# Moving GpSimd's scaling of v behind VectorE's sums, and state copies behind a bank copy, in a fused attention and MLP kernel

## The chip, the cores and the metric

One core of a Trainium2 chip runs the whole program in one launch. The metric is the device time of that core in microseconds (us); the page and the traces count from the start of the profiled span.

## The reference

A causal linear attention with a decay per head, in blocks, followed by an MLP with the exact GELU:

```python
# q, k, v: (4, 8, 768, 64); lam: (8,), 0.97 to 0.99; blocks of 64 positions
for b in range(nb):
    intra = einsum(einsum(qb, kb) * Dmask, vb)       # Dmask = lam ** (i - j) for i >= j
    inter = einsum(qb * lam_pow, kv_state)           # lam_pow = lam ** (pos + 1)
    out[block] = intra + inter
    kv_state = lam ** 64 * kv_state + einsum(kb * lam ** (63 - pos), vb)
x = out as (3072 tokens, 512)
h = x @ w_in                                         # w_in: (512, 2048)
result = gelu(h) @ w_out                             # w_out: (2048, 512)
```

## The kernel before

**Tiling.** The 768 positions of the 4 batches are cut into 24 chunks of 128 positions, numbered so that four chunks in a row are the same positions of the four batches. Four chunks make a group: group 0 to 5, each 512 tokens of the MLP. While the MLP of group g runs on TensorE, the attention of the chunks of group g + 1 is fitted in between, so that its output `xT[g + 1]` is there when the next group begins.

**The MLP of a group** (from group 1 on) saves matmuls by forming seven products where eight are needed, at the price of sums and differences. In `first_blocks`, the first layer:

- `los` and `his` are plain blocks (L643) on the low and high half of the tokens, and `x` and `y` two `Step` objects of seven products each (L426).
- Products 4 to 7 read `x_s[4]`, `x_s[1]`, `x_s[2]` and `x_s[3]`: differences of parts of x, made by `x_sums` on VectorE (L402). Both inputs of these four steps lie in SBUF.
- ScalarE copies a product's bank out (`kept`, L432), VectorE adds the next product to it from the bank (`total`, L435), ScalarE applies the GELU (L438, L646).
- A bank is used again: for instance products 6, 7 and 4 of a step go into `ha` one after the other, each behind the copy or add that reads the one before.

In `blocks_by_seven`, the second layer, products m1, m2, m5, m6, m3, m7, m4 are made twice (u = 0 and 1, L535). m1, m6, m7 and m4 use bank a; ScalarE copies it out behind m1, m6 and m7 (`f_p`, `f_u`, L567) and behind m4 (L620). `g_sum` (L516) are VectorE's sums of the GELU's outputs, again from SBUF to SBUF. The blocks m3 and m7 stand in the order m3 0, m7 0, m7 1, m3 1, m4 0.

**The attention of a pair of chunks.** Loads of k, q and v are issued on GpSimd's DMA queue (`load`, L69 and L72); k and q are transposed by DMA from SyncE's queue (`dma_transposes`, L181, L182); GpSimd scales v by powers of lam (`decay_v`, L160, giving `v_dec`). On TensorE a pair has a *visit* (`pair_visit`): first the states' part of the answer for the pair `done` (L314), then the scores (L279) and the products of k and v (L290) for the pair `asked`, then the values' part (L326) for `done`. Behind the visit VectorE adds the products to the states (`mid_states` L296, `end_states` L301), masks the scores (`mask`, L305, from PSUM into `sc_m`), scales the sum of the states (`new_states`, L240, from SBUF to SBUF) and empties the answers into x (`empty_half`, L333). ScalarE reorders some states (`reorder_states`, four copies, L229).

**What sets the order.** Every engine runs its instructions in the order in which the program lists them. The blocks of the MLP give the line of time: their cost is counted in columns that TensorE streams. Each step of the attention is put on a list with a place on that line, and before each block of the MLP everything whose place has come is issued, to all engines:

```python
            while todo and todo[0][0] <= done:
                todo.pop(0)[1]()
            run()
            done += cost
```

A place is written as group plus a part of it: `g + 4 * B` is group g and four units further. One unit B is a block of 2048 columns, such as one of `los`; a group has 29 of them. A step that waits holds back all that stands behind it on its engine. For GpSimd this means that v_decs and the loads behind them stand in one line.

In group 1 the v_decs of chunks 8, 9 and 10 are issued around the start of the group (`begin_at`), ahead of the loads of chunk 12. In groups 2 to 4 they are issued at 1 B or 7 B, with new states at 9.5 B and 10.5 B and masks at 4 B. Eight semaphores serve GpSimd's loads in turn, so a load also waits until the one eight places ahead of it has landed. The tile of v has 8 buffers, `v_dec` 6, k 10 and q 8.

Of the kernel before, what the change touches and what calls it, by code (L numbers as in the profile page):

```python
# [9 lines left out]
BF16 = mybir.dt.bfloat16  # L10
# [5 lines left out]
def kernel(  # L16
# [10 lines left out]
    nc = tc.nc  # L27

    B, H, S, D = q.shape
# [10 lines left out]
    M = 4  # L40
# [5 lines left out]
    consts = ctx.enter_context(tc.tile_pool(name="consts", bufs=1))  # L46
# [104 lines left out]
    def begin(n, early=False):  # L151
        c = Chunk()
        c.n, c.sb, c.early = n, n // M, early
        c.q, c.k, c.v = (raw.pop((n, name)) for name in "qkv")
        return c

    def decay_v(c, eng):

        c.v_dec = work_pool.tile([128, H, D], BF16, tag="vd", name="v_dec", bufs=6)
        eng.tensor_mul(c.v_dec, c.v, lam_m[:, :, None].to_broadcast((128, H, D)))  # L160
# [17 lines left out]
    def dma_transposes(c):  # L178
        c.kT = work_pool.tile([128, HP, C], BF16, tag="kT", name="kT", bufs=4)
        c.qT = work_pool.tile([128, HP, C], BF16, tag="qT", name="qT", bufs=6)  # L180
        nc.sync.dma_start_transpose(out=c.kT, in_=c.k.rearrange("p h d -> p (h d)"))  # L181
        nc.sync.dma_start_transpose(out=c.qT, in_=c.q.rearrange("p h d -> p (h d)"))  # L182
# [199 lines left out]
    def w_in_sums(*which):  # L382
        lo, hi = (w_in_t[:, :, (k0 + KW[0]) * 128:(k0 + KW[0] + NW) * 128] for k0 in (0, KH))
        for i in which:
# [3 lines left out]
                        4: lambda: (lo[:, 2:], w_in_s[2], ALU.subtract)}[i]()  # L388
            nc.vector.tensor_tensor(w_in_s[i], a, b, op=op)

    def first_blocks(g, g_t, x_t, mm1):

        TH = M * C // 2
        lo, hi = slice(0, TH), slice(TH, 2 * TH)
        x_s = {}

        def x_sums():
            for i in (1, 2, 3, 4):
                x_s[i] = sum_pool.tile([128, 2, TH], BF16, tag=f"x{i}", name=f"x_sum{i}")
                a, b = {1: lambda: (x_t[:, :2, hi], x_t[:, :2, lo]), 2: lambda: (x_t[:, 2:, hi], x_s[1]),  # L400
                        3: lambda: (x_t[:, 2:, hi], x_t[:, :2, hi]), 4: lambda: (x_t[:, 2:, lo], x_s[2])}[i]()
                nc.vector.tensor_sub(x_s[i], a, b)  # L402
# [74 lines left out]
        x, y = Step(KW[0]), Step(KW[2])  # L477
        x.behind, y.ahead = y, x

        def then_sums(run):  # L480
            def both():
                x_sums()
                run()
            return both

        los = [mm1(kf, 2, lo) for kf in (0, KH, 2, KH + 2)]
        his = [mm1(kf, 2, hi, tag) for kf, tag in ((0, "t"), (KH, "o"), (2, "t"), (KH + 2, "mh"))]
        if g > 1:
            los[2] = then_sums(los[2])
        plain = 4 * 2 * TH  # L490
        plan = [(run, plain) for run in los]
        plan += [(then_sums(x.p1) if g == 1 else x.p1, plain // 2), (his[0], plain)]
        plan += [(x.p2, plain // 2), (x.p5, plain // 2), (his[1], plain)]
        plan += [(run, plain // 2) for run in (x.p6, x.p3, y.p1, x.p7, y.p2, y.p5, y.p6, x.p4, y.p3)]
        plan += [(his[2], plain), (y.p7, plain // 2), (his[3], plain), (y.p4, plain // 2)]
# [137 lines left out]
    def mlp_blocks(g):  # L633
# [31 lines left out]
        if g > 0:  # L665
            return blocks_by_seven(g, g_t, first_blocks(g, g_t, x_t, mm1))
# [26 lines left out]
    live = {}  # L693
# [104 lines left out]
    def at(when, run):  # L798
        todo.append((place(when), run))

    def begin_at(when, n):
        def run():
            live[n] = begin(n)
            dma_transposes(live[n])
            decay_v(live[n], nc.gpsimd)
        at(when, run)

    totals = {}
# [59 lines left out]
    def visit_at(when, done, asked, *then, **how):  # L868
        at(when, lambda: visit(done, asked, **how))
        for step in then:  # L870
            w, run = when, step[0]
            if isinstance(run, float):
                w, step = run, step[1:]
            at(w, lambda step=step: step[0](*step[1:]))

    B = 2 * M * 2 * C / later

    def begun(*chunks):
        for n in chunks:
            live[n] = begin(n)  # L880
# [17 lines left out]
    visit_at(1, [], [2 * M - 2, 2 * M - 1], (masks, 2 * M - 1, 2 * M - 2),  # L898
             (w_in_sums, 4, 3), banks="t o")
    visit_at(1 + 4 * B, [2 * M - 2, 2 * M - 1], [], (empties, 2 * M - 2, 2 * M - 1), (sums, M, M + 2),  # L900
             (1 + 9.5 * B, new_states, M), (1 + 10.5 * B, new_states, M + 2), states_of=(M, M + 2), kv_tags="sc sc")
    n = 2 * M
    steps((1 + 7 * B, prefetch, 3 * M + 1), (1 + 11 * B, prefetch, 4 * M - 1),
          (1 + 15 * B, pair_visit, None, n, "t o"), (1 + 16 * B, mid_states, n), (1 + 16 * B, end_states, n),
          (1 + 16 * B, mask, n, 0), (1 + 16 * B, mask, n, 1),
          (1 + 19 * B, pair_visit, n, n + 2, "mh mo", nc.scalar.copy), (1 + 23 * B, mid_states, n + 2),
          (1 + 23 * B, end_states, n + 2), (1 + 24 * B, empty_half, n, 0), (1 + 25 * B, empty_half, n, 1),
          (1 + 25 * B, new_states, n), (1 + 25 * B, reorder_states, n + M),
          (1 + 25 * B, mask, n + 2, 0), (1 + 25 * B, mask, n + 2, 1),
          (1 + 16 * B, decayed, n + M, n + M + 1, n + M + 2, n + M + 3), (1 + 16 * B, prefetch, 4 * M),  # L910
          (1 + 26 * B, prefetch, 4 * M + 1))
    for g in range(2, NG):
        n = (g + 1) * M
        done, asked = n - 2, n if g < NG - 1 else None
        early = (g + 1 * B, empty_half, done, 0), (g + 1 * B, empty_half, done, 1)
        if not asked:
            steps((g, begin_answers, done, nc.vector.tensor_copy), (g + 1 * B, end_answers, done), *early)
            break
        v = g + 1 * B
        steps((v, pair_visit, done, asked), *[(v, *e[1:]) for e in early], (v, mid_states, asked))  # L920
        if asked < NCH - M:
            steps((v, end_states, asked), (g + 9.5 * B, new_states, asked))
        if done < NCH - M:
            steps((g + 10.5 * B, new_states, done))
            if done < N_UP:
                steps((g + 16 * B, reorder_states, done + M))
        steps((g + 4 * B, mask, asked, 0), (g + 4 * B, mask, asked, 1))
        if g > 2:
            steps((g + 7 * B, decays, n + 2, n + 3))
        if g < NG - 2:  # L930
            if g > 2:
                steps((g + 1 * B, prefetch, n + M + 1))
            steps((g + (7 if g > 2 else 1) * B, decayed, n + M, n + M + 1), (g + 8 * B, prefetch, n + M + 3),
                  (g + 26 * B, begun, n + M + 2, n + M + 3))
        done, asked = n, n + 2
# [13 lines left out]
    done = 0  # L949
# [42 lines left out]
```

## Time and profile before

| | before |
|---|---|
| runs | 201.25, 201.5, 205.04 us; median 201.5 |
| profiled execution | 202.12 us, its span 200.3 us |
| granted TensorE clock | 0.995 |
| TensorE busy | 189.9 us (95%) |
| VectorE busy | 135.4 us (68%) |
| ScalarE busy | 105.5 us (53%) |
| GpSimd busy | 111.0 us (55%) |

In the profile PE is TensorE's matmuls, DVE is VectorE, ACT is ScalarE, POOL is GpSimd and SPq SyncE's queue. A row of a time line gives start and duration in us, the engine, the line of the kernel, the operation, what it writes and reads, the shape and a count; in brackets stands how long the engine sat idle before it, and what it waited for. Neighbouring instructions of one kind are merged into one row. A row of DMA issues gives the size and the us from issue to landing.

### The profile page before, as it was taken

To read this page: it belongs to the slowest core of one execution; us is meant where nothing else is said; L and a number is where in the kernel's file an instruction comes from. 1 tells how busy PE (TensorE), PEld (TensorE's weight loads), DVE (VectorE), ACT (ScalarE), POOL (GpSimd) and SP (SyncE) were. 2 spreads that over 40 slices of the span, in tenths; PEclk is the share of its full clock that TensorE was granted. 3 is DMA by queue.
4 is the path that set the end of the run, shared out by engine and by line. 5 is a ranking of instruction groups with operands and counts; after the bars stand their busy time and mean duration, and the time that the engine had idled before them with its cause. 6 is when DMAs were issued, how large, how long until landed. Compare 5 with 4: busy or idle time off the path is not lost.

```text
span 200.3 us, 6454 instructions
## 1 busy us (share of the span) xinstructions
PE 189.9 (95%) x2800; PEld 154.3 (77%) x2804; DVE 135.4 (68%) x220; ACT 105.5 (53%) x205; POOL 111.0 (55%) x136
## 2 busy tenths in 40 slices
PE   7899999999989998899899989999999999999991
PEld 2478674455878887788798878898888898888880
DVE  3753504867888899488897499889577694555830
ACT  4954564234559614358923258812379522589221
POOL 8999973689957999499299971972000000000000
PEclk9999999999999999999999999999999999999997
DMA  4999999999999999999989999899500000500005
GB/s 113 151 174 176 200 204 201 157 212 151 133 207 134 154 137 139 142 251 143 106 53 117 158 279 139 56 104 111 213 0 5 0 3 23 190 3 0 0 3 209
DMA packets 102764, 24.81 MB, mean 124 GB/s; under 512 B 93264, under 2 KB 99920, under 8 KB 102736
## 3 DMA queue, kind: packets, MB, share of 16 engines
q0 software_dynamic: 81072, 13.38, 97.4%
q1 hardware_dynamic: 21520, 10.89, 28.6%
q8 instruction: 22, 0.36, 0.8%
q10 hardware_dynamic: 144, 0.13, 0.2%
q14 instruction: 6, 0.05, 0.1%
HBM read 27.27 MB, written 6.29 MB: 167 GB/s over the span
## 4 chain that ended last, share of the span: by engine, by line
PE 74%; DVE 12%; ACT 5%; issue 3%; DMA 3%; POOL 2%; DVEq 0%; POOLq 0%
PE h_ps L643 21%; PE a_ps L535 15%; PE o_ps L656 7%; PE c_ps L535 7%; PE ha_ps L426 6%; PE b_ps L535 3%; PE hc_ps L426 3%; DMA q_t<-in_q_dram 3%; DVE g_sum L516 2%; PE t_ps L166 2%; ACT g_t L438 2%; PE o_ps L314 2%; DVE x_sum L402 1%; DVE state L240 1%; PE hb_ps L426 1%
## 5 line engine op out<-in xcount | busy, mean ns | idle before, releaser
L643 PE MATMUL h_ps<-x_t,w_in_t 128*128 128x256 bf16 (+3 forms) x479 | 55.5, 265 | 0.3 <-DVE x_t L345 0.2
L643 PEld LDWEIGHTS <-w_in_t 128*128 128x128 bf16 x480 | 41.6, 98 | 7.3 <-DVE x_t L345 0.5
L646 ACT ACTIVATE g_t<-h_ps 128x512 bf16<-128x512 f32 (+2 forms) x59 | 34.0, 577 | 23.3 <-PE h_ps L643 23.3
L160 POOL TENSOR_TENSOR v_dec<-v_t,lam_m 128x512 bf16<-128x512 bf16 x23 | 24.7, 1108 | 20.4 <-DMA v_t<-in_v_dram 20.3
L535 PEld LDWEIGHTS <-g_sum 128*128 128x128 bf16 x368 | 31.6, 98 | 3.6 <-DVE g_sum L516 0.5
L535 PEld LDWEIGHTS <-g_t 128*128 128x128 bf16 x256 | 23.7, 98 | 4.2 <-issue 1.6
L69 POOL DMA_DIRECT2D v_t<-in_v_dram x24 | 22.1, 922 | 2.1 <-DMA w_out_t<-in_moe_w_out_dram 1.7
L535 PE MATMUL a_ps<-w_sum,g_sum 128*128 128x256 bf16 (+1 forms) x168 | 19.3, 268 | 0.2 <-DVE g_sum L516 0.2
L72 POOL DMA_DIRECT2D k_t<-in_k_dram x24 | 18.6, 798 | 0.0
L72 POOL DMA_DIRECT2D q_t<-in_q_dram x24 | 18.4, 790 | 0.0
L426 PEld LDWEIGHTS <-wi_sum 128*128 128x128 bf16 x160 | 15.6, 97 | 3.5 <-issue 1.3
L516 DVE TENSOR_TENSOR g_sum<-g_t 128x1024 bf16<-128x1024 bf16 x20 | 14.0, 724 | 4.0 <-ACT g_t L646 4.0
L656 PE MATMUL o_ps<-w_out_t,g_t 128*128 128x512 bf16 x61 | 14.5, 379 | 0.4 <-issue 0.3
L426 PEld LDWEIGHTS <-w_in_t 128*128 128x128 bf16 x120 | 11.6, 98 | 2.4 <-issue 0.7
L567 ACT COPY f_u<-a_ps 128x512 f32<-128x512 f32 (+1 forms) x12 | 6.2, 515 | 13.5 <-PE a_ps L535 13.5
L333 DVE TENSOR_TENSOR x_t<-o_ps,lam_q 128x512 bf16<-128x512 f32 x16 | 10.3, 683 | 4.4 <-PE o_ps L314 4.4
L438 ACT ACTIVATE g_t<-h_p 128x512 bf16<-128x512 f32 x20 | 12.8, 641 | 0.4 <-DVE h_p L435 0.3
L69 POOL DMA_DIRECT2D q_t<-in_q_dram x12 | 10.8, 904 | 2.9 <-DMA w_out_t<-in_moe_w_out_dram 2.9
L69 POOL DMA_DIRECT2D k_t<-in_k_dram x12 | 11.1, 922 | 2.1 <-DMA w_out_t<-in_moe_w_out_dram 1.7
L426 PE MATMUL ha_ps<-x_sum,wi_sum 128*128 128x256 bf16 x80 | 12.0, 272 | 0.0
L435 DVE TENSOR_TENSOR h_u<-h_u,hc_ps 128x512 f32<-128x512 f32 x10 | 6.8, 682 | 6.5 <-ACT h_u L432 5.1
L535 PE MATMUL a_ps<-w_sum,g_t 128*128 128x256 bf16 (+1 forms) x96 | 9.6, 255 | 1.4 <-ACT f_u L567 1.4
(110 smaller groups left out, 337.5 us busy)
## 6 DMA issues: line engine op xcount, KB each, us to landing
out_dram<-o_sb SPq DMA_DIRECT2D x9, 512.0 KB, 4.2
v_t<-in_v_dram POOLq DMA_DIRECT2D x24, 128.0 KB, 5.9
w_out_t<-in_moe_w_out_dram POOLq DMA_DIRECT2D x4, 512.0 KB, 11.0
w_in_t<-in_moe_w_in_dram POOLq DMA_DIRECT2D x7, 256.0 KB, 7.1
k_t<-in_k_dram POOLq DMA_DIRECT2D x12, 128.0 KB, 6.9
q_t<-in_q_dram POOLq DMA_DIRECT2D x12, 128.0 KB, 6.9
k_t<-in_k_dram POOLq DMA_DIRECT2D x24, 64.0 KB, 4.6
q_t<-in_q_dram POOLq DMA_DIRECT2D x24, 64.0 KB, 4.8
```

The source lines that it names most:

```text
L69: nc.gpsimd.dma_start(raw[n, name], chunk_of(name, n))
L72: nc.gpsimd.dma_start(raw[n, name][:, r::2, :], chunk_of(name, n)[:, r * HP:(r + 1) * HP, :])
L160: eng.tensor_mul(c.v_dec, c.v, lam_m[:, :, None].to_broadcast((128, H, D)))
L333: nc.vector.tensor_mul(x[:, :, :, HALVES[t]], pairs[n].o_ps[t], lam_q[:, :, None, HALVES[t]].to_broadcast((128, HP, 2, D)))
L426: nc.tensor.matmul(self.banks[b][:, k, :], left[i](q, self.kf + k), right[i](q), start=(tag is not None and k == 0 and q == 0), stop=(q == 1),
L435: nc.vector.tensor_add(self.sb[name], self.sb[name], self.banks[b])
L438: nc.scalar.activation(g_t[:, k0 + self.kf:k0 + self.kf + 2, cols], src, ACT.Gelu)
L516: nc.vector.tensor_tensor(gsum[i][:, ks, :], part(a), part(b), op=op)
L535: nc.tensor.matmul(o[:, d], left[i](k, slice(u * C, (u + 1) * C)), right[i](k)[:, d], start=(begin and k == 0 and d.start == 0), stop=(k = ...
L643: nc.tensor.matmul(h_ps[:, k, :], w_in_t[:, ki, (kf + k) * 128:(kf + k + 1) * 128], x_t[:, ki, cols], start=(k == 0 and ki == 0), stop=(ki ...
L646: nc.scalar.activation(g_t[:, kf:kf + ks, cols], h_ps, ACT.Gelu)
L656: nc.tensor.matmul(om[io], g_t[:, kf, io * C:(io + 1) * C], w_out_t[:, kf, :], start=(kf == 0), stop=(kf == NK2 - 1))
```

## The change

The sums of x are issued in two parts; v's scaling stands behind a copy on GpSimd that reads one column of the last sum; new states move from 9.5 B and 10.5 B to between the two parts of the sums; the masks of a group's first visit move behind the sums, to 9.5 B and 11 B; in group 1 the reordering copies of ScalarE move from 25 B to 26 B; the second visit's mid and end states move from 22 B to 23 B.

```diff
-        x_s = {}
-        def x_sums():
-            for i in (1, 2, 3, 4):
+        x_s = x_s_of[g] = {}
+        def x_sums(*which):
+            for i in which:
...
         if g > 1:
-            los[2] = then_sums(los[2])
+            los[2] = then_sums(los[2], 1, 2)
+            los[3] = then_sums(los[3], 3, 4)
...
-        plan += [(then_sums(x.p1) if g == 1 else x.p1, plain // 2), (his[0], plain)]
+        first_p1 = then_sums(x.p1, 1, 2) if g == 1 else x.p1
+        plan += [(first_p1, plain // 2), (then_sums(his[0], 3, 4) if g == 1 else his[0], plain)]
...
         def run():                                   # begin_at
             live[n] = begin(n)
             dma_transposes(live[n])
-            decay_v(live[n], nc.gpsimd)
...
+    gate = consts.tile([128, 1], BF16)
+    def behind_sums(g):
+        nc.gpsimd.tensor_copy(gate, x_s_of[g][4][:, 0, :1])
...
-             (1 + 9.5 * B, new_states, M), (1 + 10.5 * B, new_states, M + 2), states_of=(M, M + 2), kv_tags="sc sc")
+             (1 + 4.5 * B, new_states, M), (1 + 4.5 * B, new_states, M + 2), states_of=(M, M + 2), kv_tags="sc sc")
     n = 2 * M
-    steps((1 + 7 * B, prefetch, 3 * M + 1), (1 + 11 * B, prefetch, 4 * M - 1),
+    steps((1 + 7 * B, behind_sums, 1), (1 + 7 * B, decays, *range(n, n + M)),
+          (1 + 7 * B, prefetch, 3 * M + 1), (1 + 11 * B, prefetch, 4 * M - 1),
...
-          (1 + 25 * B, new_states, n), (1 + 25 * B, reorder_states, n + M),
+          (1 + 25 * B, new_states, n), (1 + 26 * B, reorder_states, n + M),
...
         if asked < NCH - M:
-            steps((v, end_states, asked), (g + 9.5 * B, new_states, asked))
+            steps((v, end_states, asked), (g + 3 * B, new_states, asked))
         if done < NCH - M:
-            steps((g + 10.5 * B, new_states, done))
+            steps((g + 3 * B, new_states, done))
...
-        steps((g + 4 * B, mask, asked, 0), (g + 4 * B, mask, asked, 1))
+        steps((g + 9.5 * B, mask, asked, 0), (g + 11 * B, mask, asked, 1), (g + 4 * B, behind_sums, g))
         if g > 2:
-            steps((g + 7 * B, decays, n + 2, n + 3))
+            steps((g + 4 * B, decays, n + 2, n + 3))
...
-            steps((g + (7 if g > 2 else 1) * B, decayed, n + M, n + M + 1), (g + 8 * B, prefetch, n + M + 3),
+            steps((g + 4 * B, decayed, n + M, n + M + 1), (g + 8 * B, prefetch, n + M + 3),
...
-        steps((w, pair_visit, done, asked, "mh mo", nc.scalar.copy), (g + 22 * B, mid_states, asked))
+        steps((w, pair_visit, done, asked, "mh mo", nc.scalar.copy), (g + 23 * B, mid_states, asked))
         if asked < NCH - M:
-            steps((g + 22 * B, end_states, asked))
+            steps((g + 23 * B, end_states, asked))
```

In the built programs, TensorE and SyncE have the same instructions in the same order before and after. VectorE has the same steps: in groups 1 to 4 the state steps (L240) now stand between x_sum 2 and x_sum 3, the two masks of a group's first visit stand between the adds (L435), and in groups 2 to 4 the second visit's mid and end states stand behind the last g_sum. On ScalarE only the four state copies of group 1 have moved, behind the second `f_u`. GpSimd has four additional instructions, one gate for each of the groups 1 to 4: in group 1 the loads of chunk 12 now stand in front of the gate and the four v_decs of chunks 8 to 11 behind it.

More of the change, by code (lines that the diff above doesn't have):

```diff
@@ L389, in w_in_sums @@
             nc.vector.tensor_tensor(w_in_s[i], a, b, op=op)
+    x_s_of = {}
     def first_blocks(g, g_t, x_t, mm1):
@@ L478, in first_blocks, with then_sums @@
         x.behind, y.ahead = y, x
-        def then_sums(run):
+        def then_sums(run, *which):
             def both():
-                x_sums()
+                x_sums(*which)
                 run()
```

## The prediction

> **What bounds the kernel now.** I read the page first, then what TensorE waited for, then the time lines of TensorE, VectorE, GpSimd and ScalarE in the stages where it waited. The page's span and busy row:
>
> ```profile
> span 200.3 us, 6454 instructions
> PE 189.9 (95%) x2800; PEld 154.3 (77%) x2804; DVE 135.4 (68%) x220; ACT 105.5 (53%) x205; POOL 111.0 (55%) x136
> ```
>
> TensorE is busy 95% and its 2800 matmuls stay as they are, in the same order. A change of order elsewhere can only take away TensorE's holes, or make new ones. The view of waits on TensorE names the holes behind the first group (us in total, times, longest):
>
> ```profile
> PE a_ps L535 <- ACT f_u L567: 1.4, 1, 1.4
> PE hc_ps L426 <- DVE x_sum L402: 0.9, 2, 0.6
> PE ha_ps L426 <- DVE h_p L435: 0.5, 1, 0.5
> PE a_ps L535 <- DVE g_sum L516: 0.2, 1, 0.2
> ```
>
> That is 3.0 us, and the edit touches the producer of each of the four. The view counts a little too little: a matmul's recorded end reaches 0.17 us past the start of the next one when nothing waits (109.30 + 1.04 = 110.34 against 110.17, quoted below). I add 0.17 to each wait.
>
> **Term A, group 1's first x_sum.** Time lines of the engines (start, us, engine):
>
> ```profile
> 55.88 2.08 POOL L160 TENSOR_TENSOR v_dec<-v_t,lam_m 128x512 bf16<-128x512 bf16 x2
> 57.54 0.73 DVE L402 TENSOR_TENSOR x_sum<-x_t 128x512 bf16<-128x512 bf16 x1
> 58.31 0.60 PE L426 MATMUL hc_ps<-x_sum,wi_sum 128*128 128x256 bf16 x4 [0.35 <-DVE x_sum L402]
> ...
> 88.14 0.41 DVE L402 TENSOR_TENSOR x_sum<-x_t 128x512 bf16<-128x512 bf16 x1
> 87.52 1.49 POOL L72 DMA_DIRECT2D q_t<-in_q_dram  x2
> ...
> 59.31 0.68 DVE L435 TENSOR_TENSOR h_p<-h_p,hb_ps 128x512 f32<-128x512 f32 x1
> 60.92 0.63 ACT L438 ACTIVATE g_t<-h_p 128x512 bf16<-128x512 f32 x1
> ```
>
> An x_sum alone takes 0.41 us; with GpSimd's v_dec already running it took 0.73, ending when the run of v_decs had ended (57.96) plus its own work. GpSimd issuing loads (87.52) does not stretch it. In the changed program loads of chunk 12 stand there and the four v_decs of chunks 8 to 11 come behind the gate, so x_sum saves 0.31 us of the 0.52 us hole. But the two state steps now stand between x_sum 2 and x_sum 3, and the first add of h_p, which started at 59.31, comes near 60.1 (from 57.54: two sums at 0.35, two states at 0.60, two sums at 0.34). Its GELU began at 60.92 and can now not begin before about 60.83; from there ScalarE runs without a pause and its copies free the banks. I keep 0.1 us (bounds 0 and 0.31).
>
> **Term B, the state copies behind bank a's.** End of group 1, and the same place in group 2:
>
> ```profile
> 78.53 1.04 PE L535 MATMUL c_ps<-w_out_t,g_sum 128*128 128x256 bf16 x8
> 78.69 1.65 ACT L229 COPY state<-state 64x256 bf16<-64x256 bf16 x4 [1.99 <-DVE state L240]
> 80.36 0.59 ACT L567 COPY f_u<-a_ps 128x512 f32<-128x512 f32 x1
> 80.99 1.95 PE L535 MATMUL a_ps<-w_sum,g_t 128*128 128x128 bf16 x32 [1.43 <-ACT f_u L567]
> ...
> 109.30 1.04 PE L535 MATMUL c_ps<-w_out_t,g_sum 128*128 128x256 bf16 x8
> 110.17 1.91 PE L535 MATMUL a_ps<-w_sum,g_t 128*128 128x256 bf16 x16
> ```
>
> Product 4 goes into bank a again, so it waits until ScalarE has copied bank a out (f_u). In group 1 four state copies (1.65 us) stand in front of that copy. In group 2 nothing does, and TensorE goes on 0.87 us later without a hole. The hole is 1.43 + 0.17 = 1.60 us. Moved from 25 B to 26 B, the copies follow f_u: f_u would run from 78.6 to 79.2, product 4 from 79.4, the copies from 79.2 to 80.9. What is late next: their reader is mid_states of chunk 12 on VectorE, 4 us further on, and the copy of product 4 on ScalarE, which can't start before 81.2. So the copies cost nothing where they go; if ScalarE were busy there, they would cost 1.65 us again. Bank, mask and loads are then asked for 1.6 us earlier at the next visit, which is what can eat this term:
>
> ```profile
> 61.52 1.04 POOL L160 TENSOR_TENSOR v_dec<-v_t,lam_m 128x512 bf16<-128x512 bf16 x1 [3.55 <-DMA v_t<-in_v_dram]
> 66.62 0.46 PE L290 MATMUL kv_ps<-v_dec,k_t 64*64 64x64 bf16 x32
> 61.58 0.69 DVE L435 TENSOR_TENSOR h_p<-h_p,ha_ps 128x512 f32<-128x512 f32 x1
> 54.99 0.91 POOL L69 DMA_DIRECT2D v_t<-in_v_dram  x1
> v_t<-in_v_dram POOLq DMA_DIRECT2D x1, 128.0 KB, 10.9
> 66.42 1.08 POOL L160 TENSOR_TENSOR v_dec<-v_t,lam_m 128x512 bf16<-128x512 bf16 x1
> 77.97 0.68 DVE L240 TENSOR_TENSOR state<-tmp,lam_c 128x512 bf16<-128x512 f32 x1
> 79.03 3.08 POOL L160 TENSOR_TENSOR v_dec<-v_t,lam_m 128x512 bf16<-128x512 bf16 x3
> 74.32 1.85 SPq L182 DMA_TRANSPOSE qT<-q_t  x1
> qT<-q_t SPq DMA_TRANSPOSE x1, 7.3
> 83.93 0.22 PE L279 MATMUL sc_ps<-qT,kT 64*64 64x64 bf16 x2
> ```
>
> The gate holds GpSimd's queue: behind it wait four v_decs and then the loads of chunks 13, 14 and 15. In front of it now stand the five loads of chunk 12; by the built program the last of them waits until v of chunk 10 has landed, 61.5 by the first row. So the gate is read near 62.4 and not when x_sum 4 ends (60.1), and the v_decs of chunks 8 and 9 end near 64.5; the first product that needs them stands at 66.62, a cover of 2 us. The masks and adds that VectorE runs meanwhile read PSUM: the add at 61.58 took its 0.69 us beside a v_dec. v of chunk 11 lands at 54.99 + 10.9 = 65.9, so its v_dec ends near 67.0 instead of 67.5 (66.42 + 1.08), however early the others are. The three chunks of loads behind it are as many as before, so the next v_decs come near 78.6 instead of 79.03, and k and q of chunk 13 some 0.4 us earlier than now. Their last transpose lands at 74.32 + 7.3 = 81.6; TensorE, which asked for it at 83.93, will ask at about 82.2. The cover shrinks from 2.3 to 0.6 us and holds. VectorE's state step (77.97, now about 77.6) must start ahead of the v_decs at 78.6; behind them it would wait for the whole run of three (term D shows such a wait), end near 82.2, and two masks of 0.6 us would hold the next scores until 83.4, 1.2 us. I take 1.5 us, bounds 0.3 (1.5 less 1.2) and 1.6.
>
> **Term C, the last add of group 2.**
>
> ```profile
> 93.59 1.79 DVE L240 TENSOR_TENSOR state<-tmp,lam_c_up 128x512 bf16<-128x512 f32 x1
> 93.70 1.13 POOL L160 TENSOR_TENSOR v_dec<-v_t,lam_m 128x512 bf16<-128x512 bf16 x1
> 97.11 0.68 DVE L435 TENSOR_TENSOR h_p<-h_p,ha_ps 128x512 f32<-128x512 f32 x1
> 97.83 0.60 PE L426 MATMUL ha_ps<-x_sum,w_in_t 128*128 128x256 bf16 x4 [0.50 <-DVE h_p L435]
> ```
>
> Here the state step stands beside a v_dec and takes 1.79 us where its undisturbed kind takes 0.68 (77.97). All adds behind it come late, and y's product 4 waits 0.50 + 0.17 = 0.67 us for the last of them (97.11). In the changed order both states run in front of x_sum 3, when GpSimd issues loads only, and two masks, which read PSUM, stand between the adds: as many steps in front of the last add, none of them stretched. The add then ends with its own product instead of the queue; I take 0.6 us (bounds 0 and 0.67). Were the cover gone, that is, v_decs beside the states, they would lose the 1.1 us again.
>
> **Terms D and E, group 3.**
>
> ```profile
> 115.92 3.15 POOL L160 TENSOR_TENSOR v_dec<-v_t,lam_m 128x512 bf16<-128x512 bf16 x3
> 117.04 2.32 DVE L402 TENSOR_TENSOR x_sum<-x_t 128x512 bf16<-128x512 bf16 x1
> 119.41 0.60 PE L426 MATMUL hc_ps<-x_sum,wi_sum 128*128 128x256 bf16 x4 [0.57 <-DVE x_sum L402]
> ...
> 132.95 1.13 POOL L160 TENSOR_TENSOR v_dec<-v_t,lam_m 128x512 bf16<-128x512 bf16 x1
> 131.95 2.69 DVE L516 TENSOR_TENSOR g_sum<-g_t,g_sum 128x1024 bf16<-128x1024 bf16 x2
> 137.67 1.48 PE L535 MATMUL a_ps<-w_sum,g_sum 128*128 128x256 bf16 x12 [0.17 <-DVE g_sum L516]
> ```
>
> The x_sum waits for three v_decs; behind the gate they start only after x_sum 4, beside adds and masks. The hole of 0.57 + 0.17 = 0.74 us goes: 0.7 us (bounds 0 and 0.74). The v_dec at 132.95, which stretches two g_sums, moves up behind the same gate; with the second mid and end states now behind the last g_sum, that g_sum comes earlier still. The hole of 0.17 + 0.17 = 0.34 us goes: 0.3 us (bounds 0 and 0.34). The last two v_decs move behind group 4's gate, far ahead of their first use.
>
> [...]
>
> **The gate itself** is a copy of one column, which no row of before shows on GpSimd. Its nearest rows are the v_dec of 1.04 us, its upper bound, and nothing, its lower: four of them cost 0 to 4.2 us of GpSimd's time, which is 55% busy (page). I take a quarter of a us each and nothing on the path, since in front of each gate GpSimd waits for loads or for x_sum 4 anyway. The moved masks are last read at the visit at 19 B, and at 11 B they come before that with several us to spare.
>
> **The sum.** 0.1 + 1.5 + 0.6 + 0.7 + 0.3 = 3.2 us. The profiled execution took 202.12 us, its span of 200.3 and 1.8 us around it; I forecast 198.9 for it, a span near 197.1. It lies 0.6 us above the median of the runs, 201.5. On that median's scale the forecast is **198.3 us**, 1.6% less. The upper bounds add up to 0.31 + 1.6 + 0.67 + 0.74 + 0.34 = 3.7 us; as stalls of VectorE also leave small holes behind them that no row names, I allow 4.5 us, 197.0.
>
> **The rivals.**
> Rival 1, the next visit eats B: VectorE's state step falls behind the run of v_decs at 78.6, or the transposed q of chunk 13 lands late. For it: the covers are 1.0 us (77.6 against 78.6) and 0.6 us. Against it: both sides hang on the same landing at 65.9 and move together. B shrinks to 0.3 us: 199.5 us.
> Rival 2, the change doesn't do what it says for GpSimd: v_decs wait for their loads (3.55 us at 61.52) more than for the gate, so they fall on other steps of VectorE from SBUF, the g_sums. For it: the v_dec of chunk 17 waits on a landing, not on the gate. Against it: in groups 3 and 4 the loads have landed long before. Then C, D and E bring nothing and A + B remain, 1.6 us: 199.9 us.
> Rival 3, more than my sum: holes that no row ties to one producer close too. For it: VectorE is late in all of group 3. Against it: no row names them, and a hole that has no named producer may stay. With 1.2 us more than my sum: 197.1 us.
> Rival 4, slower: loads of chunk 12, issued at 55.9 instead of 62.5, share the engines with v of chunk 11, which already takes 10.9 us to land. By X us later v_dec 11, hence the loads of chunk 13, hence its transposed q, hence TensorE at 82.2, all else waiting behind. It costs X less the cover of 0.6, so the time is 198.3 + X - 0.6, slower than before once X passes 3.8. At X = 5, five loads of about 1 us served ahead, it is 202.7 us. For it: the landings grew to 10.9 us when loads stood close together. Against it: chunk 12's loads stand behind chunk 11's in the same queue.
>
> **How the numbers follow.** Forecast 0.55, rival 1 0.12, rival 2 0.08, rival 3 0.19, rival 4 0.06. The range, 197.0 to 200.6, holds the first four with the bounds of the costs and leaves out most of rival 4 and the tails. Two per cent, about what a measurement of this kernel can tell from no change, is 4.0 us: faster means under 197.5. Rival 3 mostly reaches that, and the upper tail of my own forecast a little: 0.24. Slower by over 2% needs 205.5, so X above 7.8: 0.05. Within 2%: 0.71.
>
> **What would show it.** In the profile of the changed kernel product 4 of group 1 follows its predecessor at 0.87 us (B); no x_sum takes over 0.5 us and no state step over 0.8 (A, C, D); the four waits quoted second are gone but for some tenths; v_dec runs begin right behind the gates in groups 3 and 4. Wrong would be: a wait of TensorE on qT or on masks around 82 us, a v_dec of chunk 11 much later than 67 us, or g_sums stretched over 0.9 us that TensorE then waits for.

## The result, and the profile after

The changed kernel takes **198.4 us** (four runs, 198.36 to 198.82). Against the kernel before, run on the same chip, the ratio is **0.986, interval 0.983 to 0.988**; a second series gave 198.8 us (six runs, 197.9 to 199.3) and 0.988, interval 0.984 to 0.991. So it is 1.2 to 1.4% faster, inside the 2% to which the prediction gave 0.71; 198.3 us had been forecast. The profiled execution took 198.82 us and its span is 196.9; 198.9 and 197.1 had been forecast. (Some executions of this kernel family take up to 8 us longer than the rest; ratios leave them out, two of the four of the kernel before in the first series among them, and where a profile below is of such a one its own time is given.)

The page's span, busy row and row of instruction transfers:

```profile
span 196.9 us, 6463 instructions
PE 188.3 (96%) x2800; PEld 153.9 (78%) x2804; DVE 127.3 (65%) x220; ACT 105.1 (53%) x205; POOL 111.6 (57%) x140
...
q8 instruction: 22, 0.36, 0.7%
```

VectorE is busy 8.1 us less with the same 220 instructions, 7.3 us of it from 55 us on. There it is the steps from SBUF, x_sums, states and g_sums, that got shorter; the adds and masks, which read a bank, take what they took (means of 0.68 to 0.69 us and 0.68 us in both). TensorE's matmuls are the same. Its waits (us in total, times, longest):

```profile
PE t_ps L166 <- DMA k_t<-in_k_dram: 0.9, 1, 0.9
PE kv_ps L290 <- issue: 0.9, 2, 0.5
PE o_ps L660 <- issue: 0.3, 2, 0.2
```

The four waits of the prediction are gone. What is left stands in the kernel before too, at the start of the program and of group 1, but for one row: twice TensorE stood still amid the products of k and v without waiting for anything that the profile names ("issue"):

```profile
71.42 0.38 PE L290 MATMUL kv_ps<-v_dec,k_t 64*64 64x64 bf16 x22 [0.38 <-issue]
...
83.56 0.25 PE L290 MATMUL kv_ps<-v_dec,k_t 64*64 64x64 bf16 x6 [0.52 <-issue]
```

(The kernel before has a pause at the first of these places as well, too short for its view: 0.34 us from one product's start to the next at 71.54, against 0.57 here.)

Where the time came from is seen best at seven products of TensorE that mark the stages. The time line of the changed kernel, with the product in front of product 4 (78.46) between them:

```profile
55.25 0.61 PE L428 MATMUL ha_ps<-x_t,w_in_t 128*128 128x256 bf16 x4
57.63 0.60 PE L428 MATMUL hc_ps<-x_sum,wi_sum 128*128 128x256 bf16 x4
65.38 0.60 PE L428 MATMUL ha_ps<-x_sum,w_in_t 128*128 128x256 bf16 x4
78.46 1.04 PE L539 MATMUL c_ps<-w_out_t,g_sum 128*128 128x256 bf16 x8
79.33 1.95 PE L539 MATMUL a_ps<-w_sum,g_t 128*128 128x128 bf16 x32
96.14 0.60 PE L428 MATMUL ha_ps<-x_sum,w_in_t 128*128 128x256 bf16 x4
116.80 0.60 PE L428 MATMUL hc_ps<-x_sum,wi_sum 128*128 128x256 bf16 x4
135.79 0.38 PE L539 MATMUL c_ps<-w_out_t,g_sum 128*128 128x256 bf16 x2
```

Of the kernel before, those of the seven that the prediction does not show:

```profile
55.62 0.61 PE L426 MATMUL ha_ps<-x_t,w_in_t 128*128 128x256 bf16 x4
65.81 0.60 PE L426 MATMUL ha_ps<-x_sum,w_in_t 128*128 128x256 bf16 x4
138.99 0.38 PE L535 MATMUL c_ps<-w_out_t,g_sum 128*128 128x256 bf16 x2
```

And of a second profile of the changed kernel (span 196.7 us), whose group 1 began later:

```profile
56.05 0.61 PE L428 MATMUL ha_ps<-x_t,w_in_t 128*128 128x256 bf16 x4
58.43 0.60 PE L428 MATMUL hc_ps<-x_sum,wi_sum 128*128 128x256 bf16 x4
66.19 0.60 PE L428 MATMUL ha_ps<-x_sum,w_in_t 128*128 128x256 bf16 x4
79.72 1.95 PE L539 MATMUL a_ps<-w_sum,g_t 128*128 128x128 bf16 x32
95.88 0.60 PE L428 MATMUL ha_ps<-x_sum,w_in_t 128*128 128x256 bf16 x4
116.63 0.60 PE L428 MATMUL hc_ps<-x_sum,wi_sum 128*128 128x256 bf16 x4
135.63 1.04 PE L539 MATMUL c_ps<-w_out_t,g_sum 128*128 128x256 bf16 x8
```

Each execution counted from the first of the seven, the start of group 1, which the change doesn't touch; the lead is the time before less the time after (for instance 80.99 - 55.62 = 25.37 before, 79.33 - 55.25 = 24.08 after, lead 1.29):

| up to | edit behind it | lead, first profile | lead, second profile |
|---|---|---|---|
| first x_sum product, group 1 | A | 0.31 | 0.31 |
| last product of y, group 1 | A | 0.06 | 0.05 |
| product 4 of group 1 | B | 1.29 | 1.70 |
| last product of y, group 2 | C | 1.32 | 2.38 |
| first x_sum product, group 3 | D | 2.24 | 3.21 |
| second c product, group 3 | E | 2.83 | 3.79 |
| end of the span | | 3.03 | 4.03 |

The steps between two rows differ from B to D: the first profile lost time there in the two pauses, the second has no such pause. Both spans end nearly alike, since the second started group 1 0.8 us later. The prediction's sum of 3.2 lies between the two. The hole of term B itself is closed alike in both: product 4 follows its predecessor after 0.87 and 0.88 us (78.46 and 79.33; in the second profile 78.84 and 79.72), where it took 2.46 us before (78.53, 80.99), so 1.58 to 1.59 us less.

The other engines of the first profile, at the edits' places:

```profile
57.95 1.29 DVE L240 TENSOR_TENSOR state<-tmp,lam_c 128x512 bf16<-128x512 f32 x2
60.54 0.63 ACT L440 ACTIVATE g_t<-h_p 128x512 bf16<-128x512 f32 x1 [0.33 <-DVE h_p L437]
60.03 0.20 POOL L885 COPY gate<-x_sum 128x1 bf16<-128x1 bf16 x1
60.17 3.04 POOL L160 TENSOR_TENSOR v_dec<-v_t,lam_m 128x512 bf16<-128x512 bf16 x3
63.40 1.04 POOL L160 TENSOR_TENSOR v_dec<-v_t,lam_m 128x512 bf16<-128x512 bf16 x1 [0.18 <-PE hc_ps L428]
...
78.66 0.59 ACT L571 COPY f_u<-a_ps 128x512 f32<-128x512 f32 x1 [2.03 <-PE a_ps L539]
79.14 1.65 ACT L229 COPY state<-state 64x256 bf16<-64x256 bf16 x4
76.30 3.54 POOL L160 TENSOR_TENSOR v_dec<-v_t,lam_m 128x512 bf16<-128x512 bf16 x3
77.23 0.70 DVE L240 TENSOR_TENSOR state<-tmp,lam_c 128x512 bf16<-128x512 f32 x1
```

The two states of group 1 (57.95) and x_sum 4 behind them are done when the gate is read at 60.03, and the run of v_decs follows 0.14 us later. In ScalarE's line f_u now stands ahead of the four state copies, and product 4 (79.33) follows it at once. The run of v_decs at 76.30 came ahead of the state step at 77.23, the order that the prediction feared; yet that step took 0.70 us.

### The profile page after: what moved, and what is told of

Its sections match the earlier page's. It is cut to its first block, busy times and chain, and to the rows that moved or that the text cites. A ratio compares the mean times of both kernels' runs of the same rounds, so it can differ in the third digit from the quotient of the medians.

```text
span 196.9 us, 6463 instructions
## 1 busy us (share of the span) xinstructions
PE 188.3 (96%) x2800; PEld 153.9 (78%) x2804; DVE 127.3 (65%) x220; ACT 105.1 (53%) x205; POOL 111.6 (57%) x140
## 4 chain that ended last, share of the span: by engine, by line
PE 91%; ACT 4%; DMA 2%; issue 1%; DVE 1%
PE h_ps L647 26%; PE a_ps L539 18%; PE c_ps L539 9%; PE ha_ps L428 9%; PE o_ps L660 7%; PE hc_ps L428 5%; PE b_ps L539 4%; PE hb_ps L428 2%; PE o_ps L314 2%; DMA lam_b<-in_lam_dram 2%; PE kv_ps L290 1%; PE t_ps L166 1%; PE o_ps L326 1%; PE sc_ps L279 1%; PE o_ps L255 1%
## 5 line engine op out<-in xcount | busy, mean ns | idle before, releaser
L160 POOL TENSOR_TENSOR v_dec<-v_t,lam_m 128x512 bf16<-128x512 bf16 x23 | 24.1, 1066 | 6.0 <-DMA v_t<-in_v_dram 5.7
L520 DVE TENSOR_TENSOR g_sum<-g_t 128x1024 bf16<-128x1024 bf16 x20 | 13.1, 691 | 4.3 <-ACT g_t L650 4.3
L885 POOL COPY gate<-x_sum 128x1 bf16<-128x1 bf16 x4 | 0.8, 196 | 20.1 <-DVE x_sum L404 20.1
```

What stands on the lines that cost most here:

```text
L520: nc.vector.tensor_tensor(gsum[i][:, ks, :], part(a), part(b), op=op)
```

## Experiments

**1. The changed kernel again.** The same program in a series of its own, beside experiments 5, 6 and the second part of 8.

> The changed kernel itself, as the measure for the kernels beside it. Both theories: ratio to the kernel before 0.983 to 0.988. If its pauses of TensorE for instructions (0.38 us at 71.4, 0.52 us at 83.6) hang on where the blocks of 256 instructions end, and not on chance, they stand again at the same two places of the program, 0.3 to 0.8 us each.

Measured: 0.988 [0.984, 0.991]; its profile is the second one above. The longest pause of TensorE that is put down to instructions is under 0.25 us: neither of the two stood again. So how long TensorE stands there differs between executions of one program (0.57 and 0.72 us from start to start in the first, under 0.25 in the second), and the theory that the place alone decides falls.

**2. The state copies alone (term B).** Before, with one edit:

```diff
-          (1 + 25 * B, new_states, n), (1 + 25 * B, reorder_states, n + M),
+          (1 + 25 * B, new_states, n), (1 + 26 * B, reorder_states, n + M),
```

> The kernel before with one edit: the four state copies of group 1 at 26 B instead of 25 B. My theory (term B alone, 1.6 us, less what the next visit gives back): the wait of product 4 in group 1 goes, and the median falls by 1.0 to 1.6 us, to a ratio of 0.992 to 0.995. TensorE reaches the next visit without a pause and stops for about 0.5 us in the products of k and v with nothing named, as in the changed kernel; the holes of groups 2 and 3 (x_sum, h_p, g_sum) stay. Rival: the copies' move does nothing alone, because the masks or loads of the next visit hold TensorE until the same time: a ratio of 0.998 to 1.002.

Measured: 0.998, interval 0.995 to 1.000. A hole of 1.6 us is 0.8% of the time; 0.2% came out, which can't be told from nothing and is what the rival had. In the profile (200.61 us) the hole is closed as in the changed kernel: product 4 comes 0.87 us behind its predecessor (77.91, 78.78), a lead of 1.59 us. By the end of the visit that follows 1.15 us of it was lost again. The time lines of VectorE and GpSimd and TensorE's wait show where:

```profile
77.27 3.73 DVE L240 TENSOR_TENSOR state<-tmp,lam_c 128x512 bf16<-128x512 f32 x1
77.28 3.16 POOL L160 TENSOR_TENSOR v_dec<-v_t,lam_m 128x512 bf16<-128x512 bf16 x3
PE kv_ps L290 <- ACT o_sb L620: 0.6, 1, 0.6
```

The state step, which alone takes 0.68 us, was held for the run of three v_decs, and the masks and copies behind it came late at the next visit. That is rival 1 of the prediction, in the kernel without the gate. In this profile step and run began within 0.01 us of each other; in the changed kernel's first profile the run began 0.93 us ahead of the step, which slipped in between the first v_dec and the second. The run came early there, and so did the loads ahead of it: the v_dec in front of them ended at 64.44 and not at 65.80.

**3. The gate and the state copies, without moved states and masks.** The changed kernel, with

```diff
-             (1 + 4.5 * B, new_states, M), (1 + 4.5 * B, new_states, M + 2), ...
+             (1 + 9.5 * B, new_states, M), (1 + 10.5 * B, new_states, M + 2), ...
-            steps((v, end_states, asked), (g + 3 * B, new_states, asked))
+            steps((v, end_states, asked), (g + 9.5 * B, new_states, asked))
-            steps((g + 3 * B, new_states, done))
+            steps((g + 10.5 * B, new_states, done))
-        steps((g + 9.5 * B, mask, asked, 0), (g + 11 * B, mask, asked, 1), ...
+        steps((g + 4 * B, mask, asked, 0), (g + 4 * B, mask, asked, 1), ...
```

> The changed kernel with new states and masks back at their old places (9.5 and 10.5 B, 4 B); the gate, the split sums, the copies at 26 B and the later mid states stay. My theory: the v_decs behind the gate now stand beside the states, which lie from SBUF to SBUF; state steps of 1.2 to 4 us appear in groups 1 and 3, TensorE waits 0.5 to 2 us for adds behind them, and the time is 0.5 to 2.5 us above the changed kernel: 198.9 to 200.9, ratio 0.988 to 0.997. Rival (the gate alone is what helps, the moved states and masks nothing): the same time as the changed kernel within 0.3 us, 198.1 to 198.7.

Measured: 0.989, interval 0.985 to 0.994, so most of the gain is there. But of its seven times only three lie at 199.0 to 201.0; the others are 202.7 to 205.8 us, and the profile is one of these, 203.65 us. For a second profile:

> The gate and the state copies of the change, with states and masks at their old places, once more. Theory: near 199.2 us; the state steps of group 1 may meet the v_decs behind the gate, and where one is held for 3 us the time is near 203. The states of group 2 run beside a v_dec or not, so term C (TensorE waiting 0.3 to 0.7 us for the last add of group 2) shows here if it hangs on the moved states. Rival (the gate alone brings C): no wait of TensorE for h_p at 96 to 98 us.

That execution took 203.4 us. VectorE and GpSimd in group 1:

```profile
61.46 3.64 DVE L240 TENSOR_TENSOR state<-tmp,lam_c 128x512 bf16<-128x512 f32 x1
61.50 3.04 POOL L160 TENSOR_TENSOR v_dec<-v_t,lam_m 128x512 bf16<-128x512 bf16 x3
```

At their old places the states of group 1 come behind the gate, beside the very run that it releases; TensorE then waited 2.4 us for the h_p behind the held state, and 2.1 us for a g_sum that the run of the next visit held (78.69; the pair of g_sums at 77.00 took 5.40 instead of 1.29); from 68.0 to 71.4 us its granted clock was 0.50, of which experiment 4 shows more. In group 2 both states took 0.68 us and TensorE waited for no h_p. So term C does not hang on the moved states once the gate holds the v_decs back: there the rival held. (Nor does it need the gate: see experiment 7.) What the moved states are worth is that in group 1 they stand ahead of the gate.

**4. No gate.** The changed kernel without the four copies:

```diff
-    steps((1 + 7 * B, behind_sums, 1), (1 + 7 * B, decays, *range(n, n + M)),
+    steps((1 + 7 * B, decays, *range(n, n + M)),
-        ... (g + 11 * B, mask, asked, 1), (g + 4 * B, behind_sums, g))
+        ... (g + 11 * B, mask, asked, 1))
```

> The changed kernel without the four gate copies; all else, the place of the v_decs in GpSimd's order too, as in the changed kernel. My theory: in groups 3 and 4 GpSimd no longer stands for 5.3 and 14.8 us, the v_decs of group 3 start near 112.7, run for about 4 us and catch x_sum 1 at 115.2 for 1 to 1.6 us, a hole of 0 to 0.8 us on TensorE in front of hc; in groups 1 and 2 the order and the loads alone keep the v_decs where they are. The time is 0.3 to 1.0 us above the changed kernel: 198.7 to 199.4. Rival (the place in the order is enough, the gate does nothing): the same within 0.2 us.

Measured: 0.987, interval 0.983 to 0.990, from two executions at 199.2 and 199.3 us; the two others took 204.9 and 206.1, and the profile is of the last:

```profile
57.96 4.10 DVE L404 TENSOR_TENSOR x_sum<-x_t 128x512 bf16<-128x512 bf16 x1
58.66 3.11 POOL L160 TENSOR_TENSOR v_dec<-v_t,lam_m 128x512 bf16<-128x512 bf16 x3
62.12 1.01 PE L428 MATMUL hc_ps<-x_sum,wi_sum 128*128 128x256 bf16 x4 [3.73 <-DVE x_sum L404]
```

The first x_sum was held until three v_decs had ended, though by the record the first of them began 0.7 us behind it; TensorE waited 3.7 us. The expectation had named group 3 for this and held group 1 safe. And the wait is not the whole price: the four products behind it took 1.01 us instead of 0.60, and from 61.2 to 68.0 us the granted clock of TensorE was 0.50, where the changed kernel has 1.00. Against the kernel before, counted as in the table above, TensorE was 3.4 us behind at this product and 6.3 us at the last product of y. For a second profile:

> The kernel without gates once more, one look. Theory (bistable in group 1): either a time near 199.3 us with x_sum 1 of group 1 at 0.4 to 0.8 us, or one near 205 us with an x_sum or state step of group 1 held for 3 us or more. Rival (the long time comes from elsewhere): near 205 us with all steps of VectorE in group 1 under 1.3 us.

Here it was x_sum 59.09 with 3.58 us, TensorE waiting 2.4 us for it and 1.4 us for a g_sum held by the next run, and the execution took 202.3 us; the granted clock stayed at 1.00 behind the wait. Both profiles show the held step in group 1, as the theory had it; they do not show an undisturbed one.

**5. The gate one pair of sums earlier.** It reads x_sum 2:

```diff
-        nc.gpsimd.tensor_copy(gate, x_s_of[g][4][:, 0, :1])
+        nc.gpsimd.tensor_copy(gate, x_s_of[g][2][:, 0, :1])
```

> The changed kernel with the gate reading x_sum 2 instead of x_sum 4, so that the runs of v_decs may begin two sums earlier and x_sums 3 and 4 and the state steps stand beside them. Theory (a step of VectorE from SBUF that comes during a run of v_decs is held until the run ends): where v has landed, in groups 3 and 4, x_sum 3 takes 2 to 4 us instead of 0.41 and TensorE waits for it or for the adds behind it, 1.5 to 3 us in each; time 201 to 204 us. Rival (VectorE is held for one v_dec, 1 us, at most, as the state step of the next visit was): no x_sum over 1.2 us, TensorE waits under 0.8 us in each group, 198.5 to 200 us.

Measured: 205.55 us, one execution. The time line:

```profile
58.97 3.41 DVE L404 TENSOR_TENSOR x_sum<-x_t 128x512 bf16<-128x512 bf16 x1
59.06 3.04 POOL L160 TENSOR_TENSOR v_dec<-v_t,lam_m 128x512 bf16<-128x512 bf16 x3
123.26 1.26 DVE L404 TENSOR_TENSOR x_sum<-x_t 128x512 bf16<-128x512 bf16 x1
124.44 1.26 DVE L404 TENSOR_TENSOR x_sum<-x_t,x_sum 128x512 bf16<-128x512 bf16 x1
```

The time was worse than the theory's, and the place another: the whole run held x_sum 3 in group 1, which the expectation had not named, and in groups 3 and 4 x_sums lost one v_dec at most, as the rival had it. TensorE waited 2.2 us for the held x_sum, 1.6 us for a g_sum behind the next run, and from 64.2 to 67.6 us its granted clock was 0.50. So both happen on this pair of engines: the steps that begin with a run lose the run, and one that comes amid a run may get in after one v_dec or lose the rest of the run (the x_sums of 2.32 us in the prediction's term D and of 2.70 us in experiment 7).

**6. Group 1's states behind the first add**, meant to win term A back:

```diff
-             (1 + 4.5 * B, new_states, M), (1 + 4.5 * B, new_states, M + 2), ...
+             (1 + 6 * B, new_states, M), (1 + 6 * B, new_states, M + 2), ...
```

> The changed kernel with group 1's two state steps one step later, behind the first add of h_p, instead of in front of x_sum 3. Theory (term A was lost because the two state steps push the add, and with it ScalarE's first GELU, back): TensorE's lead at the last product of y in group 1 keeps the 0.3 us that it has at the first x_sum product, and the time is 0.3 us (0.1%) below the changed kernel's, about 198.1 on the scale of 198.4. Rival (the block of instructions that TensorE needs right behind that place comes no earlier): the lead is there at 65 us, the pause at 71.4 grows by as much, and the time is the changed kernel's within 0.1 us.

Measured: four executions at 198.2 to 199.4 us, eight at 200.7 to 206.2; ratio 0.989, interval 0.984 to 0.994, from the five shortest. The 0.3 us can't be told, and the edit opens what the change had closed, as the profile of an execution of 204.8 us shows:

```profile
59.09 4.84 DVE L240 TENSOR_TENSOR state<-tmp,lam_c 128x512 bf16<-128x512 f32 x2
59.74 3.04 POOL L160 TENSOR_TENSOR v_dec<-v_t,lam_m 128x512 bf16<-128x512 bf16 x3
```

TensorE waited 3.4 us for the add behind the held states, and from 64.3 to 67.7 us its granted clock was 0.50. Term A's 0.25 us is the price for both states being done when the gate opens.

**7. The gate of group 1 alone.** The changed kernel without the gates of groups 2 to 4 (the second edit of experiment 4).

> The changed kernel with the gate of group 1 alone; the gates of groups 2, 3 and 4 are left out, their v_decs stay where the change puts them. Theory (the long times of the kernel without any gate, 205 to 206 us, come from group 1, where a step of VectorE from SBUF is held for a whole run of v_decs, 3 to 4 us, when the run starts just ahead of it): all runs between 197.9 and 199.6 us, no x_sum of group 1 over 0.5 us, and the hole of term D stays closed, since the v_decs are moved behind the sums in GpSimd's order too. Rival (the gates of groups 3 and 4 carry D and E): an x_sum of group 3 takes 2 us or more, TensorE waits 0.5 us or more for it, and the time is 0.7 to 1.0 us above the changed kernel's, 199.1 to 199.8.

Measured: 0.988, interval 0.986 to 0.991; nine of eleven runs at 198.9 to 199.6 us, the two others, against the theory, at 202.0 and, the profiled one, 200.63 us. Group 3:

```profile
114.96 3.19 POOL L160 TENSOR_TENSOR v_dec<-v_t,lam_m 128x512 bf16<-128x512 bf16 x3
115.75 2.70 DVE L404 TENSOR_TENSOR x_sum<-x_t 128x512 bf16<-128x512 bf16 x1
118.50 0.60 PE L428 MATMUL hc_ps<-x_sum,wi_sum 128*128 128x256 bf16 x4 [0.94 <-DVE x_sum L404]
```

Theory and rival each had half. With the gate in group 1 no x_sum or state there was held. Without the gate of group 3 term D is back, the same step caught by the same run, 0.94 us. (As much again, 0.9 us, went in an unnamed pause, kv_ps <- issue, at 72.44.) The ratio alone doesn't tell this kernel from the changed one; the wait does. In both profiles of experiment 4, also without that gate, the step caught nothing or little there: the x_sum took 0.42 and 0.80 us. So with the v_decs moved down GpSimd's list alone it hangs on the time at which they run; with the copy that reads the last sum it doesn't.

In group 2, without its gate, both states took 0.68 to 0.69 us, ahead of the v_dec at 92.98, and TensorE waited for no h_p: term C is closed here by the moved states alone, as it was by the gate alone in experiment 3.

**8. Instructions of TensorE.** The two unnamed pauses asked for a cause. Each ended 2.7 to 2.9 us after one of the page's 22 instruction transfers began, of 16 KB (0.36 MB by 22). If they hang on blocks of instructions, more instructions at the start move them:

```diff
-    keep_warm(12, cols=480)
+    keep_warm(48, cols=120)
```

(36 idle products more, 72 instructions with their weight loads, as many columns as before.)

> The changed kernel with 48 warming matmuls of 120 columns at the very start instead of 12 of 480: the same columns, 72 more instructions on TensorE ahead of everything. Theory (the pauses of 0.4 and 0.5 us that the trace names nobody for, in the products of k and v of the visits in groups 1 and 2, come when TensorE's next block of instructions is not there yet): the pauses move to other instructions, by about 36 matmuls earlier, and may fall where matmuls are long enough to hide them; the median lies 0.9 us below to 0.1 above the changed kernel. Rival (they come from data that arrive then, a load or a scaled v): they stay at the same matmuls, 10 and 26 into the products, with the same length.

Measured: 1.013, interval 1.008 to 1.018, 205.2 us. The pauses moved, and grew far past what was expected. Waits and time line:

```profile
PE c_ps L539 <- issue: 4.7, 3, 2.4
PE hb_ps L428 <- issue: 1.0, 1, 1.0
75.78 0.38 PE L539 MATMUL c_ps<-w_sum,g_sum 128*128 128x256 bf16 x2 [2.44 <-issue]
```

Count TensorE's instructions in the trace: each weight load and the product that it belongs to in turn, with the four products that the record lacks (x2800 against x2804 weight loads), all early, and the semaphore instructions of TensorE. Then TensorE paused when 1984, 2496, 3008 and 4032 were behind it here, 1728 and 2240 in the changed kernel, 1728 in the kernel before. All leave 192 when divided by 256: the pauses stand at one fixed place in a count of 256, as they would where blocks of 256 end. The transfers of the changed kernel's first profile give the same size: they began at 68.52, 75.13 and 80.88, the pauses ended 2.90 us behind the first of these and 2.68 behind the last, and 512 instructions lie between the pauses, so 256 to a transfer. They are called pauses for instructions here; that TensorE waits for the transfer itself is the author's reading. Behind the longest pause the granted clock was 0.50 from 76.9 to 80.3 us, as behind held steps.

Then a shift by 16, for which the changed kernel's time line gave where blocks are used up fast:

```diff
-    keep_warm(12, cols=480)
+    keep_warm(20, cols=288)
```

> The changed kernel with 16 more instructions on TensorE at its start (20 idle products of 288 columns for 12 of 480: as many columns), so that every block of 256 instructions ends 16 instructions earlier in the program. Theory (a block that TensorE uses up in less than about 5.3 us ends in a pause that makes up the difference): from the changed kernel's time line the blocks then use 4.7 us at 70.5, 5.8 at 82, 4.5 at 103.7 and 4.3 at 132, so the pause at 83.6 us goes or falls under 0.2 us, that at 71.4 stays at 0.4 to 0.9 us, and two new ones of 0.5 to 1.2 us come near 104 and 132; in sum 1.0 to 2.0 us slower than the changed kernel, 199.4 to 200.4 on the scale of 198.4. Rival (the pauses come from DMA traffic at that time and not from where a block ends): both pauses stay where they are, none near 104 and 132, and the time is within 0.3 us of the changed kernel's.

Measured: 198.65 us, 0.989, interval 0.982 to 0.996. From start to start, where 0.11 us is usual and 0.01 among the small products of k and v, TensorE stood 0.34 us behind instruction 1728, 0.23 behind 1984, 0.40 behind 2240 and 0.51 behind 4032, all at the same place in the count of 256; the changed kernel's first profile has 0.57 at 1728 and 0.72 at 2240 by this measure. The last comes near what was expected for it, that at 2240 fell by half, none came at 3008, and the time is the changed kernel's. The places are shown; what sets their length isn't. The time in which 256 instructions are used up was the author's estimate, and one length of four, that at 4032, came as expected from it.

## Why the prediction was right

The time, the sum and the direction came out, and the mechanisms of A, B, C and D with them. That the sum came out so closely in the first profile (3.03 against 3.2) is in part luck: D and E brought 0.5 us more than was taken for them, the end of the span 0.2 us, and 0.9 us went in group 1 around the pauses for instructions, which no term held. By steps:

- **A, 0.1 taken of 0.31.** Right, and for the reason given. The first x_sum product leads by 0.31, and the two states then push the adds until ScalarE waits for one (0.33 at 60.54): 0.05 is left at the end of y. Experiment 6 shows what the states would cost elsewhere.
- **B, 1.5 taken.** Right: the hole itself closed by 1.58 to 1.59 in both profiles and in experiment 2's. The steps of the table, 1.23 and 1.65, hold pauses for instructions besides, longer or shorter than before. That so much of it stayed hung on more than was written. The prediction put the cover of the next visit at 1.0 us, the state step ahead of the run; both came in the other order (76.30 and 77.23), and the step was spared all the same, by 0.1 us: it began at the end of the first v_dec, and the second, beside it, took 1.53 instead of 1.04. Rival 1 was worth more than the 0.12 that it got: without the gate it is what happened (experiment 2). What was late next was not transposed q, as feared, but the products of k and v: in the first profile 0.57 us of the lead went in the pause at 83.56.
- **C, 0.6 taken.** Right: from the start of group 2 to its last product of y the lead grows by 0.60 in both profiles (0.72 to 1.32, 1.78 to 2.38); the table's 0.03 of the first profile is that less the pause of 0.57. The reason was right too, but not the only one: no state stood beside a v_dec, and for that the moved states are enough (experiment 7), and so is the gate (experiment 3).
- **D, 0.7, and E, 0.3.** Right for D: 0.92 and 0.83 from there, 0.74 of it the named hole, and in experiment 7, without the gate of group 3, it is back. E's step gained 0.59 and 0.58, 0.34 of it the named hole and the rest in holes of group 3 that no row had named, which is rival 3 in small. That the edit closed E's named hole is not shown: the hole is gone in the profiles of experiments 2 and 7 too, of which the first has no edit in group 3 and stretched g_sums as before (130.65, two in 2.39 us). So it may come and go between executions.
- **The gate itself** took 0.20 us, as the estimate of a quarter. It opened at 60.0 and not at 62.4, and v of chunk 11 had landed by 63.4 and not at 65.9: the step that moved chunk 12's loads ahead was taken too dearly, and rival 4, which is built on later landings, had nothing to stand on here.
- **x_sums and states.** None over 0.43 and 0.70 in the first profile; in the second one state took 1.32 beside a v_dec with no wait of TensorE behind it. The groups of VectorE, in the changed kernel and then before:

```profile
L404 DVE TENSOR_TENSOR x_sum<-x_t 128x512 bf16<-128x512 bf16 x10 | 4.2, 416 | 0.0
L520 DVE TENSOR_TENSOR g_sum<-g_t,g_sum 128x1024 bf16<-128x1024 bf16 x10 | 6.4, 683 | 0.0
...
L402 DVE TENSOR_TENSOR x_sum<-x_t 128x512 bf16<-128x512 bf16 x10 | 6.4, 640 | 0.0
L516 DVE TENSOR_TENSOR g_sum<-g_t,g_sum 128x1024 bf16<-128x1024 bf16 x10 | 7.8, 824 | 0.0
```

- **The rest of a run, or one v_dec.** The prediction took from term D's row that a caught step loses the rest of the run. That and the loss of one v_dec are both seen: 4.10, 3.73, 3.64 and 3.41 us where a step met the start of a run of three, and in the midst of one 2.32 and 2.70, the rest of the run, but also 1.26, one v_dec. What tells these apart is not shown.

What stays open: whether held steps in group 1 also lengthen some executions of the kernel before (205.0 and 206.2 us in its first series). No profile of such a one was taken, and for the variants it was.

## What to carry to other kernels

When runs of one engine hold up steps of another, as the v_decs did here (steps of 0.42 and 0.68 us took 3.3 to 4.1), write down every step of the one that falls into the other's runs, and hold the run back by a copy that reads the last of those steps: a place in the list is only an order on one engine, while the gate also holds when a load lands early. Put behind the gate only what doesn't mind (here adds and masks, 0.67 to 0.69 us beside the runs), and in front of it what would be caught, even at a price of some tenths. And when a hole on the bounding engine is closed, ask what used that hole: here one hole closed alone gave back most of its worth, 1.15 of 1.59 us. Count a long wait of the bounding engine for more than its length, too, when a lower clock comes with it, as here in five of six profiles (0.50 for 3.4 to 6.8 us).

## What the runs showed of the hardware

Runs of three v_decs of 1.04 us on GpSimd held one VectorE step from SBUF of 0.42 or 0.68 us for 3.3 to 4.1 us (experiments 2 to 5), in one profile a step that by the record began 0.7 us before the run; adds and masks that read a bank took 0.67 to 0.69 us beside such runs. Six profiles of experiments 3 to 6 have a wait of 2.2 to 3.7 us of TensorE behind a held step. In five of them the granted clock stood at 0.50 for 3.4 us, or 6.8 us with the longest, beginning between 0.9 us ahead of the wait's end and 1.8 us behind it; in one, with a wait of 2.4 us, it stayed at 1.00. What decides is not shown. The page has 22 instruction transfers of 16 KB, and TensorE's pauses without a releaser in the profile stood at one place in a count of 256 of its instructions; in four of them (71.42 and 83.56 in the changed kernel, 75.78 and 92.40 in experiment 8) it went on 2.4 to 2.9 us after a transfer had begun. Seventy-two instructions more at the start, with no column more to compute, moved the pauses and took the ratio from 0.988 to 1.013, with 5.7 us of such pauses in the profile. One program had 0.9 us of them in one profile and none over 0.25 us in another.
